# Gated linear attention into a gated MLP: three weight buffers, smaller batch buffers, ScalarE copies as fp32 words and a new order table

## The chip, the cores and the metric

The kernel runs on one core of a Trainium2 chip. A core has five engines with an instruction queue each: TensorE (PE in the profile; its weight loads are PEld), VectorE (DVE), ScalarE (ACT), GpSimd (POOL) and SyncE (SP), which here issues the transfers between HBM and SBUF. Matmul results go to PSUM, eight banks of 128 x 2 KB, which POOL does not read. The metric is the time of one execution on the device in microseconds (us); the kernel before takes 141.49 us, the median of three runs (141.25 to 141.82).

## The reference

Two stages in sequence, all inputs and outputs fp32. The shapes are batch 4, 8 heads, 768 steps, head width 48; then model width 384 and hidden width 1024.

```python
state = np.zeros((B, H, D, D))
for t in range(S):
    state = alpha[:, :, t, :, None] * state + np.einsum('bhd,bhe->bhde', k[:, :, t], v[:, :, t])
    y[:, :, t] = np.einsum('bhd,bhde->bhe', q[:, :, t], state)
x = y.transpose(0, 2, 1, 3).reshape(B, S, H * D)

h = np.maximum(x @ w_in, 0.0)
u, v = h[..., :512], h[..., 512:]
v_n = (v - mean(v)) / np.sqrt(var(v) + 1e-06)
v_s = np.einsum('ts,bsd->btd', w_spatial, v_n) + b_spatial[None, :, None]
out = (u * v_s) @ w_out
```

## The kernel before, in words

The steps are cut into 24 chunks of 128, six for each batch. Chunks 0 to 7 are worked on as four pairs (function `pair`), with even and odd steps interleaved; chunks 8 to 23 one at a time (function `first`). For a chunk or pair the work is:

- four loads, alpha, k, q and v (`ac`, `kc`, `qc`, `vc`; L432 for pairs, L637 for single chunks), each into one of three buffers;
- the logarithm of alpha on ScalarE (`lnp`, L443), its running sum as matmuls with triangular matrices (`cump`, L452, two matmuls for each half of a pair), the exponentials of the sum with both signs on ScalarE (L460, L469), k and q times these (`ktp`, L474, on POOL or VectorE; `qtp`, L481, on VectorE);
- transposes of k and q on TensorE (`tr`, L502, four 128-column matmuls each) and copies of the result from PSUM to the tile `kqT` on ScalarE or VectorE (`ev`; the copies of all steps are in the helper `copy`, L198 for ScalarE and L200 for the others);
- the update of the state from k and v on TensorE (`updq`, L536 and L544), the state itself on VectorE and POOL (`z`, `S`, `sb`);
- the scores (`sc`, L574), their masking on VectorE (`m`, L585 for pairs, L756 for single chunks), the output y as scores times v (`ya`, L601) plus q times state (`y`, L614);
- a copy of y to bf16 (`xs`), its transpose (`xt`, L365 for pairs, L389 for single chunks) and the copy to `xT` (`xe`). In the pairs' `xe` the copy also puts the interleaved steps back in order, by a strided access.

The MLP stage works on a batch. `second_v` makes the six v tiles (three matmuls of 512 columns each, relu on ScalarE, statistics on VectorE at L884 and L885, then `rs` and the normalisation `vn`, L916); `second_u` makes uT; `second_s` multiplies by the transposed spatial weights `w_spT` (six matmuls of 384 columns for each of eight groups, L967 adds the bias, L980 multiplies by u); `second_o` multiplies by w_out and stores. All its matmuls are recorded at L819, in the helper `mm`.

The weights arrive as fp32 in raw buffers (`raw_w`, `NRAW` = 2), through `fetch`: a load waits until the buffer used `NRAW` loads before has been cast to bf16. w_in comes as two loads, w_spatial as three, w_out as one. w_spatial is then transposed on TensorE (`wt`, L831) and copied to `w_spT` (`we`).

The order of all the work is fixed in advance: each operation is entered in a list with a number, and `replay` emits them as the string `PLAN` says. A word is an engine letter and a number, so the table also fixes which engine does an operation that two engines could do. Each engine works through its own queue in this order. Words like `P126:512:512:512` put filler in front of a matmul operation: matmuls of 512 fp32 columns each on the constant tile `junk` (L188) that write to the PSUM bank which the operation is about to overwrite. The old table has 3,768 such columns, all in the first 20 us: 1,216 ahead of the first `cump`, 1,536 ahead of the first `tr`, then 504 and 512.

PSUM banks are taken in turn by a counter (`bank`), so an operation also waits for the readers of the bank taken eight turns before. The lines that the change touches:

```python
    NRAW, NROW, KEEP = 2, 3, 11
...
                copy(eng, bt[b]["xT"][:, c].rearrange("p k (t two) -> p k t two", two=2),
                     st["xv"].rearrange("p k (two t) -> p k t two", two=2))
...
        d["xT"] = batch.tile([128, NCH, KS, C], BF16, name="xT")
        d["uT"] = batch.tile([128, NDS, S], BF16, name="uT")
        d["v_sb"] = batch.tile([128, NT, DH], BF16, name="v_sb", bufs=2)
```

The pool `batch` has three buffers where a tile does not name another number.

## Time and profile before

| | |
|---|---|
| median of three runs | 141.49 us (141.25 to 141.82) |
| span of the profiled execution | 144.3 us (the page gives no other time for it) |
| TensorE busy | 136.8 us, 95% |
| VectorE busy | 118.7 us, 82% |
| ScalarE busy | 106.8 us, 74% |
| POOL busy | 86.8 us, 60% |
| HBM traffic | 28.64 MB, 198 GB/s |
| chain that ended last, by engine | PE 78%, DVE 8%, ACT 5%, DMA 3% |

The profile is of one execution, and its span goes from the first to the last instruction; it is 2.8 us longer than the median of the runs. In a row of a group stand the line, the engine, the tiles (written <- read), the count, then the busy time, the mean of one in ns, and the idle time ahead of them with what ended it. In a row of the timeline stand the start, the duration, the engine and line, and in brackets the idle time before it. In a row of the stretches stand, after the stretch and its length, the busy time of PE, PEld, DVE, ACT and POOL with the number of instructions, then the granted TensorE clock, the share of the transfer engines and GB/s. A matmul's duration includes its way through the array and overlaps with the next; how fast TensorE gets on is read from the starts, or from the chain.

### The profile page before, as it was taken

Reading aid. Unit: us, or ns where it says so; the run is one execution under the profiler, and the core shown is the slowest. Engines: PE = TensorE matmul, PEld = TensorE weight load, DVE = VectorE, ACT = ScalarE, POOL = GpSimd, SP = SyncE. Lnnn points to the kernel's source line nnn. Section 1 sums busy time; section 2 is a strip of 40 time slices with the busy share of each in tenths; the row PEclk is TensorE's granted clock in tenths of the full one; section 3 lists DMA queues with packets and bytes.
Section 4 is the critical chain, followed back from the end, with each engine's and each line's share of the span. In section 5 each row is a group of like instructions: output and inputs, shape, how many; then the busy total and the mean of one; then the engine's idle time right before and its main releaser. Section 6 shows DMA issues by size and latency. Waiting matters only on the chain.

```text
span 144.3 us, 4963 instructions
## 1 busy us (share of the span) xinstructions
PE 136.8 (95%) x1915; PEld 84.2 (58%) x1915; DVE 118.7 (82%) x289; ACT 106.8 (74%) x278; POOL 86.8 (60%) x152
## 2 busy tenths in 40 slices
PE   7799999799799999999999999999999999999990
PEld 3334766656465765676556665665657666555560
DVE  7015798899999969899999999999979897987940
ACT  3473479899895879899997789998797698861031
POOL 6856179892709979981249789511599687002820
PEclk9999999999999999999999999999999999999998
DMA  4999999929899989999899899799999241090055
GB/s 108 321 326 351 282 250 325 344 58 259 181 269 191 300 164 182 205 181 214 169 211 222 175 174 185 152 204 196 212 239 227 66 172 55 0 354 28 5 191 191
DMA packets 89000, 28.64 MB, mean 198 GB/s; under 512 B 83728, under 2 KB 87440, under 8 KB 88976
## 3 DMA queue, kind: packets, MB, share of 16 engines
q1 hardware_dynamic: 88944, 28.32, 79.5%
q8 instruction: 15, 0.25, 0.7%
q14 instruction: 9, 0.07, 0.1%
q0 software_dynamic: 32, 0.00, 0.0%
HBM read 23.60 MB, written 4.72 MB: 196 GB/s over the span
## 4 chain that ended last, share of the span: by engine, by line
PE 78%; DVE 8%; ACT 5%; DMA 3%; issue 3%; SPq 0%; ACTq 0%; DVEq 0%
PE bank L819 47%; PE bank L188 4%; DMA ac<-in_alpha_dram 3%; PE bank L710 3%; PE bank L452 2%; PE bank L502 2%; PE bank L745 2%; PE bank L574 2%; DVE ptm L756 2%; PE bank L773 2%; PE bank L731 2%; PE bank L544 1%; DVE ptm L585 1%; PE bank L657 1%; PE bank L601 1%
## 5 line engine op out<-in xcount | busy, mean ns | idle before, releaser
L819 PE MATMUL bank<-w_spT,vn 128*128 128x384 bf16 x192 | 36.3, 326 | 0.1
L980 POOL TENSOR_TENSOR gT<-vsb,uT 128x384 bf16<-128x384 f32 x28 | 25.7, 927 | 11.7 <-DVE vsb L967 11.2
L335 POOL TENSOR_TENSOR state<-state,bc 128x192 f32<-128x192 f32 x20 | 10.3, 513 | 21.4 <-DVE state L328 6.2
L819 PEld LDWEIGHTS <-vn 128*128 128x128 bf16 x192 | 17.1, 97 | 10.2 <-issue 0.2
L756 DVE TENSOR_TENSOR ptm<-bank,mask 128x512 bf16<-128x512 f32 x32 | 20.8, 682 | 1.0 <-ACT xT L198 1.0
L819 PE MATMUL bank<-xT,w_in 128*128 128x384 bf16 x96 | 19.4, 326 | 0.0
L967 DVE TENSOR_TENSOR vsb<-bank,bsp_bc 128x384 f32<-128x384 f32 x31 | 16.7, 554 | 3.2 <-PE bank L819 2.8
L819 PE MATMUL bank<-w_in,xT 128*128 128x512 bf16 x72 | 18.8, 379 | 0.0
L198 ACT COPY kqT<-bank 128x512 bf16<-128x512 bf16 x24 | 13.6, 590 | 6.9 <-PE bank L502 4.4
L819 PE MATMUL bank<-w_out_sb,gT 128*128 128x384 bf16 (+1 forms) x100 | 18.4, 320 | 0.1
L681 POOL TENSOR_TENSOR kt<-kc,binv 128x384 bf16<-128x384 f32 x13 | 12.0, 927 | 6.6 <-ACT bc L676 2.7
L200 POOL CAST sbd<-state 64x192 bf16<-64x192 f32 x40 | 13.6, 341 | 2.1
L884 DVE BATCH_NORM_STATS2 stats<-v_sb 128x6 f32<-128x512 bf16 x20 | 13.6, 681 | 0.5 <-ACT v_sb L204 0.5
L204 ACT ACTIVATE v_sb<-bank 128x512 bf16<-128x512 f32 x20 | 11.9, 608 | 1.6 <-PE bank L819 1.6
L198 ACT CAST x_sb<-bank 128x384 bf16<-128x384 f32 x21 | 10.2, 493 | 3.5 <-PE bank L773 2.7
L819 PEld LDWEIGHTS <-w_in 128*128 128x128 bf16 x96 | 8.7, 97 | 6.0
L188 PE MATMUL bank<-junk 128*128 128x512 f32 (+2 forms) x16 | 11.1, 838 | 1.1 <-DVE halves_of L264 1.1
L200 DVE COPY kqT<-bank 128x512 bf16<-128x512 bf16 x24 | 9.2, 415 | 3.1 <-PE bank L502 2.3
L819 PEld LDWEIGHTS <-gT 128*128 128x128 bf16 x100 | 8.7, 97 | 5.1 <-POOL gT L980 0.2
L204 ACT ACTIVATE uT<-bank 128x384 bf16<-128x384 f32 x23 | 11.3, 495 | 0.3 <-PE bank L819 0.2
L198 ACT COPY xT<-bank 128x192 bf16<-128x192 bf16 (+1 forms) x27 | 9.1, 378 | 2.4 <-PE bank L365 1.5
L585 DVE TENSOR_TENSOR ptm<-bank,mask 128x512 bf16<-128x512 f32 x16 | 10.2, 682 | 0.7 <-PE bank L574 0.4
(128 smaller groups left out, 285.2 us busy)
## 6 DMA issues: line engine op xcount, KB each, us to landing
ac<-in_alpha_dram SPq DMA_DIRECT2D x16, 192.0 KB, 3.9
kc<-in_k_dram SPq DMA_DIRECT2D x16, 192.0 KB, 4.2
qc<-in_q_dram SPq DMA_DIRECT2D x16, 192.0 KB, 4.0
vc<-in_v_dram SPq DMA_DIRECT2D x16, 192.0 KB, 3.8
raw_w<-in_moe_w_spatial_dram SPq DMA_DIRECT2D x3, 768.0 KB, 4.5
out_dram<-raw_w SPq DMA_DIRECT2D x11, 192.0 KB, 2.0
out_dram<-o_sb SPq DMA_DIRECT2D x9, 192.0 KB, 1.9
ac<-in_alpha_dram SPq DMA_DIRECT2D x4, 384.0 KB, 5.5
```

What stands on the lines that cost most here:

```text
L188: nc.tensor.matmul(out=flat[:, 0:cols].rearrange("p (a b) -> p a b", a=4), lhsT=junk, rhs=junk[:, None, 0:n].to_broadcast([128, 4, n]), st ...
L198: nc.scalar.copy(out=out, in_=in_)
L200: ENG[eng].tensor_copy(out=out, in_=in_)
L204: nc.scalar.activation(out=out, in_=in_, func=AF.Relu)
L335: ENG[eng].tensor_tensor(out=st["state"], in0=st["state"], in1=st["bc"][:, :, None].to_broadcast([128, HP, D]), op=ALU.mult)
L585: nc.vector.tensor_tensor(out=st[f"ptm{par}"][:, s], in0=st[f"pt{s}{par}"], in1=mask2[:, par], op=ALU.mult)
L681: ENG[eng].tensor_mul(out=k_blocks(kt3)[:, :, :, 0:D], in0=quad(st["kc"]), in1=st["binv"])
L756: nc.vector.tensor_tensor(out=st["ptm"][:, s], in0=st[f"pt{s}"], in1=mask4, op=ALU.mult)
L819: return lambda ps: nc.tensor.matmul(out=out(ps), lhsT=lhsT(), rhs=rhs(), start=start, stop=stop)
L884: nc.vector.bn_stats(out=stats, in_=d["v_sb"][:, tt, :])
L967: nc.vector.tensor_tensor(out=hold["vs"], in0=ps[:, 0:TH], in1=bsp_bc[:, th, :], op=ALU.add)
L980: ENG[eng].tensor_tensor(out=bt[b]["gT"][:, dsl, cols], in0=hold["vs"], in1=bt[b]["uT"][:, dsl, cols], op=ALU.mult)
```

## The change

Six things change together.

1. The weights have three raw buffers instead of two (`NRAW` = 3).
2. `xT` and `uT` have two buffers instead of three. The v tiles are no longer held as six to a batch in two buffers but as pairs, in five buffers (`v_tile`, `NVS` = 5). The dependencies follow: a copy to `xT` now waits for the v and u matmuls of two batches before, a v tile for the normalisation of the pair five pairs before, uT for the products of two batches before. uT is taken at its first use.
3. Copies of transposed blocks on ScalarE (kqT, xT, w_spT) see both sides as fp32, half as many elements; on VectorE they stay bf16 (`copy_pairs`).
4. A second, permuted identity `ident_q` is made on POOL at the start. The pairs' `xt` uses it, so that the transpose puts the steps in order and the copy to `xT` is contiguous.
5. The bias row `b_sp_sb` lies in the memory of `w_spT`'s first row.
6. The order table is another one. It has 273 words for ScalarE (257 before), 244 for VectorE (257), 116 for POOL (119), and the same 300 for TensorE and 111 for SP. Of 48 kqT copies ScalarE has 38 (24 before). The filler has 2,496 columns: 960 ahead of the first `cump`, 128 and 256 ahead of the bias matmuls, 320 ahead of the first `tr`, then 128, 192, 128, 320 and 64.

```diff
 PLAN = """
-D0 S49 Q50 D7 D13 S109 Q110 G47 Q48 D11 S51 Q52 G9 D3 S55 Q56 D1 G8 D15 D17 G14 D6 D4 D2 D12 G16 S53 Q54 A57 S113 Q114
-G18 A117 P118:512:512:192 S111 Q112 P68 A119 P262 A69 P58 S19 Q20 P264 G71 A59 P128 A120 A60 G61 S115 Q116 A70 D62
-A129 D72 A265 D5 S178 Q179 A263 D122 A130 P126:512:512:512 D132 S180 Q181 G131 P76 P74 P64 P66 D75 G63 A65 D77 G73 D67
...
+S109 Q110 D0 D15 D3 G47 Q48 D6 D2 G16 D17 S49 Q50 D13 D1 D4 D5 S51 Q52 G14 D12 A117 S113 Q114 G9 P118:320:192:384:64
+A57 S53 Q54 P264:128 A119 P58 A120 P68 S55 Q56 A59 A69 D61 P262:256 A60 P128 G71 S111 Q112 D122 A263 A70 P126:320 G18
+A265 D72 S115 Q116 A129 D62 A130 P76 P74 D132 P66 A73 S178 Q179 G63 P64 D11 A127 G8 P78 A77 A67 A75 S182 Q183 G121 D80
...
 """
...
+    NVS = 5
...
-    NRAW, NROW, KEEP = 2, 3, 11
+    NRAW, NROW, KEEP = 3, 3, 11
...
+    def copy_pairs(eng, out, in_):
+
+        copy(eng, *((out.bitcast(FP32), in_.bitcast(FP32)) if eng == "ACT" else (out, in_)))
...
-    b_sp_sb = consts.tile([1, S], BF16, name="b_sp_sb")
     wsp_nat = [None] * NT
     w_spT = consts.tile([128, NT, NT, 128], BF16, name="w_spT")
+    b_sp_sb = w_spT[0:1, 0].rearrange("p n t -> p (n t)")
...
+    def x_users(b):
+
+        return got(*[("v", b - 2, t, "mm", 0) for t in range(NT)],
+                   *[("u", b - 2, ft, th, "mm", 0) for ft in range(NDS) for th in range(2)])
...
-                    nc.tensor.transpose(xv[:, ks, :], st["x_sb"][:, ks, :], ident)
+                    nc.tensor.transpose(xv[:, ks, :], st["x_sb"][:, ks, :], ident_q)
...
-                copy(eng, bt[b]["xT"][:, c].rearrange("p k (t two) -> p k t two", two=2),
-                     st["xv"].rearrange("p k (two t) -> p k t two", two=2))
+                copy_pairs(eng, bt[b]["xT"][:, c], st["xv"])
...
-                        copy(eng, st["kT"][:, par], hold["t"])
+                        copy_pairs(eng, st["kT"][:, par], hold["t"])
...
-        d["xT"] = batch.tile([128, NCH, KS, C], BF16, name="xT")
-        d["uT"] = batch.tile([128, NDS, S], BF16, name="uT")
-        d["v_sb"] = batch.tile([128, NT, DH], BF16, name="v_sb", bufs=2)
+        d["xT"] = batch.tile([128, NCH, KS, C], BF16, name="xT", bufs=2)
...
+    def v_tile(b, tt):
+
+        k = ("v_sb", tt // 2)
+        if k not in bt[b]:
+            bt[b][k] = batch.tile([128, 2, DH], BF16, name="v_sb", bufs=NVS)
+        return bt[b][k][:, tt % 2]
+
+    def v_users(b, tt):
+
+        n = b * NT // 2 + tt // 2 - NVS
+        return got(*[("vn", 2 * n // NT, 2 * n % NT + x) for x in range(2)]) if n >= 0 else []
...
+    def c_id(_):
+        make_identity(nc, ident)
+        nc.gpsimd.tensor_copy(
+            out=ident_q.rearrange("p (t a) -> p a t", a=2), in_=ident.rearrange("p (a t) -> p a t", a=2))
```

On SP the loads of the start change their order. Before: alpha of pair 0, alpha 1, k 0, v 0, q 0, q 1, k 1, the second half of w_in, v 1, the four loads of pair 2, alpha 3, the first half of w_in, q 3, k 3, then w_spatial with the loads of chunks 8 and 9. After: alpha 1, alpha 0, k 0, q 1, q 0, v 0, k 1, v 1, the four loads of pair 2, alpha 3, the second half of w_in, q 3, the first half of w_in, k 3, two of the three loads of w_spatial, q of chunk 8, v 3.

On TensorE the old order has the first two v groups after the first chunk's `xt`, ahead of pair 2's transposes; the new order has pair 2's transposes, scores and updates first and the v groups after. Of the last operations, the old table has both halves' last copies of the output on ScalarE and a 96 KB store as the last transfer; the new one splits the last copies over ScalarE and VectorE, and the last transfer has 192 KB.

More of the change, by code (lines that the diff above doesn't have):

```diff
@@ L210 @@
     ident = consts.tile([128, 128], BF16, name="ident")
+    ident_q = consts.tile([128, 128], BF16, name="ident_q")
     mask4 = consts.tile([128, 4, 128], BF16, name="mask4")
@@ L867, in evac @@
             if not on_act:
[L868 removed]
+                relu(eng, v_tile(b, tt), ps)
                 return
             nc.scalar.activation(
[L871 removed]
+                out=v_tile(b, tt), in_=ps, func=AF.Relu, accum_out=d["sums"][:, 0, tt:tt + 1])
         Q = 1000.0 + 100 * b
         group(("v", b, tt), mms, 0.22, made[("xe", b * NCH + tt)] + made[("w_in", 1)], Q + tt, evac,
[L875 removed]
+              {"ACT": 0.61 if on_act else 0.48}, None, v_users(b, tt), parts=1)
         def bn(_):
@@ L916, in vn @@
                     nc.vector.tensor_scalar(
-                        out=d["vn"][:, t, :], in0=d["v_sb"][:, t, :],
+                        out=d["vn"][:, t, :], in0=v_tile(b, t),
                         scalar1=d["mvs"][:, t, 0:1], scalar2=d["rstd"][:, t:t + 1],
@@ L925, in vn @@
                 nc.gpsimd.tensor_scalar(
-                    out=d["vn"][:, t, :], in0=d["v_sb"][:, t, :], scalar1=d["rstd"][:, t:t + 1], scalar2=nb,
+                    out=d["vn"][:, t, :], in0=v_tile(b, t), scalar1=d["rstd"][:, t:t + 1], scalar2=nb,
                     op0=ALU.mult, op1=ALU.add)
@@ L938, in evac @@
         def evac(eng, ps):
+            if "uT" not in bt[b]:
+                bt[b]["uT"] = batch.tile([128, NDS, S], BF16, name="uT", bufs=2)
             relu(eng, bt[b]["uT"][:, ft, th * TH:(th + 1) * TH], ps[:, 0:TH])
```

120 lines of the change are left out of this document (59 added, 61 removed).

## The prediction

> **What bounds the kernel now.** I read the busy times by stretch first, then the chain that ended last, then the single instructions of the start. The columns are PE, PEld, DVE, ACT and POOL busy.
>
> ```profile
> 6.40:16.90 10.50, 10.50 (x57) 4.63 (x57) 3.90 (x11) 4.73 (x11) 5.49 (x8) 1.00 1.14 331
> 16.90:42.50 25.60, 23.61 (x523) 16.08 (x520) 24.04 (x53) 22.58 (x56) 16.19 (x30) 1.00 0.83 239
> 42.50:140.80 98.30, 98.04 (x1342) 61.46 (x1332) 88.03 (x208) 75.88 (x208) 60.20 (x97) 1.00 0.77 174
> ```
> ```profile
> 6.38 1.44 PE bank L452 x4
> 7.82 0.43 PE bank L848
> ...
> 9.42 0.75 PE bank L452 x2
> 10.17 4.25 PE bank L188 x6
> 14.43 1.12 PE bank L502 x20
> 15.55 0.90 PE bank L188 x2
> ...
> 17.35 0.18 PE bank L536 x8
> 17.53 0.51 PE bank L544 x32
> 18.03 0.35 PE bank L574 x16
> ...
> 123.54 17.18 PE bank L819 x105
> ```
>
> Three regimes follow. From 42.5 us, where the spatial matmuls (L819, from w_spT and vn) begin, to 140.8 us TensorE is full: the last 105 matmuls take 17.18 us, 164 ns each. From 16.9 to 42.5 VectorE is the tight one, 24.04 of 25.60 us, and TensorE has holes of 2 us. Before 16.9 the chain is a latency chain in which TensorE is kept busy with filler: L188, matmuls on `junk` whose result nobody reads, stands on it with 4.25 and 0.90 us.
>
> The filler's length matters, for these rows show TensorE at half rate in the first stage:
>
> ```profile
> 1.06 4.42 PE L188 MATMUL bank<-junk 128*128 128x512 f32 x6 [1.06 <-DVE halves_of L264]
> 6.97 0.84 PE L452 MATMUL bank<-la,le_pair 128*128 128x384 bf16 x2
> 28.94 0.49 PE L452 MATMUL bank<-la,le_pair 128*128 128x384 bf16 x2
> ```
>
> The same two matmuls take 0.84 us at 6.97 and 0.49 at 28.94, though the granted clock is 1.00 throughout. The first filler, 1,216 columns by the order table, takes 4.42 us, 3.6 ns a column; the one at 15.55, 504 columns, 0.90 us, 1.8 ns a column. So the full rate comes between 10.2 and 14.4 us, during the second filler of 1,536 columns (at 3.6 ns it would be 5.5 us; it took 4.25, so it turned at about 13).
>
> **The change part by part.** *Copies as fp32 words.*
>
> ```profile
> L198 ACT COPY kqT<-bank 128x512 bf16<-128x512 bf16 x24 | 13.6, 590 | 6.9 <-PE bank L502 4.4 <-PE bank L710 2.1 <-DVE w_row L200 0.4
> L200 DVE COPY kqT<-bank 128x512 bf16<-128x512 bf16 x24 | 9.2, 415 | 3.1 <-PE bank L502 2.3 <-ACT o_sb L198 0.5
> L198 ACT COPY raw_w<-bank 128x384 f32<-128x384 f32 x9 | 4.4, 484 | 0.8 <-PE bank L819 0.7 <-issue 0.2
> L198 ACT COPY raw_w<-bank 128x192 f32<-128x192 f32 x1 | 0.3, 325 | 0.0
> L198 ACT COPY xT<-bank 128x192 bf16<-128x192 bf16 x19 | 5.3, 335 | 0.9 <-PE bank L389 0.9
> ```
>
> On ScalarE 192 elements take 325 ns as fp32 and 335 as bf16, 384 fp32 take 484: time goes by elements, 0.83 ns each, not bytes. A 512-element copy becomes 256 words: 325 + 64 x 0.83 = 378 ns instead of 590. VectorE keeps its form and 415 ns. The order table uses that: of 48 kqT copies ScalarE takes 38 (24 before), VectorE 10. ScalarE: 38 x 378 - 24 x 590 = +0.2 us, VectorE -14 x 415 = -5.8 us; with the other moved operations I count ScalarE -4.4, VectorE -3.1, POOL -3.3 us over the run. After 42.5 us this is worth nothing by itself: TensorE hides it. If words were no cheaper, ScalarE would have +8 us instead (a rival).
>
> *Transposes with ident_q.* Same number of matmuls, and the pair chunks' xT copy becomes contiguous. It costs POOL one 128x128 copy at the start; nearest is this POOL row, 661 ns for 512 elements, so between 0.17 (128 elements at its rate) and 0.66 us; I take 0.3, nearer the small end by size:
>
> ```profile
> L241 POOL TENSOR_SCALAR_AFFINE_SELECT mask<-mask 64x512 bf16<-64x512 bf16 x4 | 2.6, 661 | 0.1
> ```
>
> It is hidden: POOL's first ktp needs ScalarE's exponential, after 8 us. POOL now also makes one mask (two selects, 1.3 us) ahead of the triangles that the first cumulative sum needs; they were done at 4.1 us and will be at about 4.5, under the 5.1 at which it can start; without that cover 0.4 us.
>
> *Buffers.* Five pairs of v tiles instead of six, xT and uT for two batches instead of three: a v tile now waits for the normalisation (vn) five pairs back, xT for the matmuls of two batches back. By both order tables at least 27 us of TensorE work lie between, so nothing; without that distance ScalarE's v copy, and the copies queued behind it, would wait. The bias row shares w_spT's space and is read some 30 us before w_spT is written: nothing.
>
> *Third weight buffer and the loads' order.*
>
> ```profile
> 18.46 1.29 SPq L1084 DMA_DIRECT2D raw_w<-in_moe_w_in_dram  x1
> 31.77 0.37 SPq L1084 DMA_DIRECT2D raw_w<-in_moe_w_spatial_dram  x1
> raw_w<-in_moe_w_in_dram SPq DMA_DIRECT2D x2, 768.0 KB, 6.5
> ```
>
> The second w_spatial load held SP's queue until 31.77 for a free buffer, with the last v of the pairs behind it; now it waits for the first w_in casts, on VectorE at about 25, so the queue moves on some 5 us sooner. In return the first w_in load goes from 8th to 14th, behind pair 2's four loads and pair 3's alpha. It is issued at about 18.46 less its own share of the stream (768 KB at 331 GB/s, 2.4 us) = 16.1 and lands 6.5 later, 22.6, ahead of its casts. Pair 2's inputs come 2.4 us earlier.
>
> *The new order at the start.* The filler is 2,496 columns instead of 3,768, in smaller pieces.
>
> ```profile
> 4.24 0.84 ACT L443 ACTIVATE la<-ac 128x768 bf16<-128x768 f32 x1 [2.21 <-DMA ac<-in_alpha_dram]
> 5.48 0.84 ACT L443 ACTIVATE la<-ac 128x768 bf16<-128x768 f32 x1 [0.40 <-DMA ac<-in_alpha_dram]
> 16.89 1.29 DVE L585 TENSOR_TENSOR ptm<-bank,mask 128x512 bf16<-128x512 f32 x2 [0.33 <-issue]
> ```
>
> The alpha pair that TensorE needs first is now loaded first: its logarithm ends at 5.08, not 6.32. Then, at half rate: sums of that pair 0.72 (half of the L452 x4) to 5.8; filler of 128 at 3.6 ns 0.46, bias 0.43, to 6.7; the other pair's four 1.44 to 8.1; filler 256 0.92, bias 0.43, two sums 0.75, to 10.2; filler 320 1.15, to 11.4. There the first transposes start, 14.43 before. Five of them, 0.22 at full rate (1.12/5), 0.44 at half, end at 13.6; the update matmuls 0.18 + 0.51 at 14.3; then ScalarE's small exponential and its last copy, 0.2 + 0.38, 14.9; the first scores 0.35, 15.3: the first mask on VectorE at 15.3 instead of 16.89, 1.6 us sooner. ScalarE carries all of these copies, four were VectorE's: at 0.38 they keep up.
>
> From the first mask to the first spatial matmul VectorE then has, by the order table and the spacing of each group in the trace, 13 masks (2.48/4 = 0.62) 8.1, six statistics 0.80 each 4.8, four qt 2.05, four vn 1.9, four state sums 1.3, two u 1.0, two copies 0.7, two w_in casts 0.9, x_sb 0.53, kt 0.52, w_spT 0.3: 22.1 us, against 24.04 busy in 25.60 before. The rows for masks and vn:
>
> ```profile
> 28.86 2.48 DVE L585 TENSOR_TENSOR ptm<-bank,mask 128x512 bf16<-128x512 f32 x4 [0.39 <-PE bank L574]
> 35.28 1.92 DVE L916 TENSOR_SCALAR vn<-v_sb,mvs,rstd 128x512 bf16<-128x512 bf16 x4
> ```
>
> With the same share of holes it takes 22.1 x 25.60/24.04 = 23.5 us, 2.1 less. So the spatial matmuls start between 1.6 us earlier (only the first mask's lead survives) and 1.6 + 2.1 = 3.7 us. I take 2.5, near the middle, because the second half of each pair's masks now waits for scores that stand later in TensorE's order, which may eat about half of the 2.1. Late next is TensorE itself.
>
> *From there on* the matmuls are the same: nothing, within 2 us either way. *The tail:*
>
> ```profile
> 140.75 0.70 ACT L198 COPY raw_w<-bank 128x384 f32<-128x384 f32 x2 [0.17 <-PE bank L819]
> 141.67 0.41 SPq L1011 DMA_DIRECT2D out_dram<-raw_w  x1
> out_dram<-raw_w SPq DMA_DIRECT2D x2, 96.0 KB, 1.7
> out_dram<-raw_w SPq DMA_DIRECT2D x11, 192.0 KB, 2.0
> ```
>
> Two ScalarE copies in 0.70 become one of 0.48 beside one of VectorE, -0.2; the last store has 192 KB instead of 96, +0.3: nothing.
>
> **Sum.** Span 144.3 - 2.5 = 141.8. The profiled span stands 2.8 us over the median of 141.49 (page and runs give no other time for that execution), so I scale: 2.5 x 141.49/144.3 = 2.45, 139.0 us.
>
> **The rivals.** *The clock stays at half.* Without the 1,536 columns there is no unbroken stretch of 4.25 us; if the full rate came only at about 20 us, the work from 13 to 20 would go at half: up to the first y that is two updates (1.4), three transposes (0.7), three scores (1.05) and a pair's sums (0.7), 3.8 us at full rate, and so 3.8 us more; 142.8. It decides if the rate turns after about 18 us. For it: 4.42 us of filler at 1.06 did not turn it. Against it: 6.4 to 11.4 is now as closely filled as before, and when TensorE is late it is busy, which turns it. The Trainium skill, "TensorE: Matmul & The Clock Gate", Part 1, speaks for it: the full clock needs a busy window of about 3.4 us, and the window runs freely. By that rule any gap in the window can cost another one, and the sum would be the rival's 142.8 rather than 139.0. The trace agrees in so far as 4.42 us of filler, followed by a gap, left the next matmuls at half rate. Chance 0.16.
>
> *VectorE takes it all back.* The masks, statistics and vn before the first spatial matmul wait for each other; if holes of 2.5 us open there, 141.4. For it: VectorE is the tight engine there. Against: it has 2 us less to do. Chance 0.12.
>
> *ScalarE becomes the bound.* If words cost what bf16 elements did, 212 ns each: its 14 kqT copies before the spatial matmuls are 3.0 us, six pair xT and four w_spT copies at 155 ns 1.5; 4.5 on an engine with 25.60 - 22.58 = 3.0 to spare: the lead of 2.5 lost and 1.5 over, 143.0, and with 24 more such copies later, each 0.2 where TensorE has no slack, up to 145; 144. Against: the 192-element rows. Chance 0.08.
>
> *The middle gains too.* These are the best spacings of a chunk's matmuls:
>
> ```profile
> 53.04 0.19 PE bank L389 x6
> 53.23 0.23 PE bank L710 x16
> 54.71 0.33 PE bank L745 x8
> 58.33 0.20 PE bank L731 x8
> 60.15 0.17 PE bank L767 x4
> 60.32 0.20 PE bank L773 x8
> ```
>
> Sixteen chunks at 1.3 us and 0.1 for their sums are 22.5 us; 365 matmuls at 164 ns 59.9; 54 at 217 ns (0.65 for three) 11.7: 94 of the 98.3 us after 42.5. If half of the 4 us goes, 137.0. For it: loads now lead their first reader by 4.1 us or more of TensorE work, 2.8 before. Chance 0.12.
>
> **How the numbers follow.** The forecast has 0.52, own range 137.8 (all 3.7) to 140.5 (a little over 1). Half a per cent, 0.7 us, is what a measurement can tell from no change. Faster: 0.50 + 0.12 + 0.02 = 0.64; within: 0.02 + 0.08 = 0.10; slower: 0.16 + 0.08 + 0.02 = 0.26. The range 136.6 to 143.0 reaches to the middle's gain and to the half clock, and leaves out ScalarE's case and both ends.
>
> **What would show it.** Right: first transposes near 11.4, first mask near 15.3, first spatial matmul near 40; kqT copies on ScalarE at about 380 ns; from there TensorE full for 98 us. Wrong: L502 or L574 at twice their spacing after 15 us; kqT copies near 590; TensorE idle for VectorE or ScalarE after 45 us; the first w_in load landing after 25.

## The result, and the profile after

| | before | after |
|---|---|---|
| median of 20 runs each, same chip | 141.82 us (141.25 to 147.89) | 142.63 us (141.63 to 144.03) |
| ratio after / before | | 1.0064, 95% interval 1.0040 to 1.0088 |
| runs under 142 us, over 144 us | 13, 5 | 4, 1 |

By the ratio the change makes the kernel slightly slower: 0.64%, where 139.0 us had been forecast. The ratio leaves out executions more than 1.5% above the fastest of their kernel, five of before's (those over 144 us) and two of after's, so it is not the quotient of the two medians, which are over all runs. The mean of all 20 runs hardly differs (142.61 and 142.71 us): before is mostly near 141.5 us and sometimes near 145, after lies between. The profiled execution of after has a span of 140.0 us and a time of 141.79; in every run with a span on record the time is 1.7 to 1.9 us more than the span.

The page after, its busy times and the groups that answer to those of before (columns as there):

```profile
PE 132.6 (95%) x1923; PEld 84.2 (60%) x1923; DVE 118.9 (85%) x276; ACT 101.7 (73%) x294; POOL 84.5 (60%) x150
...
L199 ACT COPY kqT<-bank 128x256 f32<-128x256 f32 x38 | 13.3, 384 | 3.9 <-PE bank L720 3.2
...
L936 DVE TENSOR_SCALAR vn<-v_sb,mvs,rstd 128x512 bf16<-128x512 bf16 x24 | 11.1, 491 | 1.0 <-ACT rstd L929 0.9
```

The word copies cost what was forecast, 384 ns against 378. VectorE's busy time has not fallen (118.7 before): vn costs 491 ns where it was 430.

TensorE's timeline of after at the start. It is the counterpart of the rows of L188, L452 and L502 before (now L189, L462, L512):

```profile
1.05 3.67 PE L189 MATMUL bank<-junk 128*128 128x320 f32 x8 [1.05 <-DVE junk L1073]
5.13 0.32 PE L462 MATMUL bank<-la,le_pair 128*128 128x384 bf16 x1 [0.40 <-ACT la L453]
...
6.68 0.49 PE L462 MATMUL bank<-la,le_pair 128*128 128x384 bf16 x2
...
8.71 0.40 PE L512 MATMUL bank<-ident,qt 128*128 128x128 bf16 x4
```

Two sums of a pair take 0.49 us already at 6.68, so the full rate is there before; the profile of before had 0.84 at 6.97. The first transposes start at 8.71, not at 11.4 as forecast.

The stretches of after, cut at the first mask (12.8) and at the first spatial matmul (36.6); columns as in the prediction:

```profile
6.00:12.80 6.80, 5.47 (x91) 3.80 (x90) 4.36 (x10) 6.31 (x19) 4.31 (x8) 1.00 1.17 325
12.80:36.60 23.80, 23.33 (x485) 16.18 (x486) 22.07 (x50) 22.07 (x61) 15.40 (x29) 1.00 1.04 309
36.60:136.30 99.70, 99.21 (x1341) 61.17 (x1337) 89.88 (x201) 70.18 (x213) 60.80 (x99) 1.00 0.76 172
```

VectorE is busy for 22.07 of 23.80 us between the two marks, as forecast (22.1 of 23.5). TensorE then takes 99.7 us to its last matmul, where the profile of before had 98.5 between the same two marks. And the transfers' share is 1.04 in the middle stretch: there is no room left in it. The answers to the load rows of before:

```profile
raw_w<-in_moe_w_spatial_dram SPq DMA_DIRECT2D x3, 768.0 KB, 8.0
...
raw_w<-in_moe_w_in_dram SPq DMA_DIRECT2D x2, 768.0 KB, 7.6
```

These took 4.5 us (w_spatial, by the same view of before between 16 and 43 us) and 6.5 before.

The end of after, all engines:

```profile
126.36 5.53 PE L827 MATMUL bank<-w_spT,vn 128*128 128x384 bf16 x33
...
128.34 2.66 POOL L1003 TENSOR_TENSOR gT<-vsb,uT 128x384 bf16<-128x384 f32 x3 [11.02 <-DVE vsb L990]
...
130.15 1.26 DVE L1003 TENSOR_TENSOR gT<-vsb,uT 128x384 bf16<-128x384 f32 x1
131.33 0.55 DVE L983 TENSOR_TENSOR gT<-bank,uT 128x384 bf16<-128x384 f32 x1
...
134.34 1.97 PE L827 MATMUL bank<-w_out_sb,gT 128*128 128x384 bf16 x15 [0.34 <-DVE gT L1003]
```

One product on VectorE takes 1.26 us; three of POOL's run from 128.34 to 131.00, the last of them beside it. VectorE's next product, which reads PSUM and starts when POOL's are done, takes 0.55. Four microseconds after the slow one TensorE waits 0.34 us for VectorE's last product.

### The profile page after: what moved, and what is told of

It reads as the page before. It is cut to its first block, busy times and chain, and to the rows that moved or that the text cites. A ratio compares the mean times of both kernels' runs of the same rounds, so it can differ in the third digit from the quotient of the medians.

```text
span 140.0 us, 4956 instructions
## 1 busy us (share of the span) xinstructions
PE 132.6 (95%) x1923; PEld 84.2 (60%) x1923; DVE 118.9 (85%) x276; ACT 101.7 (73%) x294; POOL 84.5 (60%) x150
## 3 DMA queue, kind: packets, MB, share of 16 engines
HBM read 23.60 MB, written 4.72 MB: 202 GB/s over the span
## 4 chain that ended last, share of the span: by engine, by line
PE 83%; ACT 6%; DMA 3%; DVE 2%; issue 2%; POOL 1%; SPq 0%; POOLq 0%; DVEq 0%; ACTq 0%
PE bank L827 54%; PE bank L720 3%; DMA ac<-in_alpha_dram 3%; PE bank L755 3%; PE bank L667 2%; PE bank L783 2%; PE bank L584 2%; PE bank L512 2%; PE bank L741 2%; PE bank L777 2%; PE bank L399 2%; PE bank L376 1%; ACT bank L479 1%; PE bank L839 1%; ACT binvp L470 1%
## 5 line engine op out<-in xcount | busy, mean ns | idle before, releaser
L1003 POOL TENSOR_TENSOR gT<-vsb,uT 128x384 bf16<-128x384 f32 x25 | 22.5, 914 | 13.8 <-DVE vsb L990 13.3
L341 POOL TENSOR_TENSOR state<-state,bc 128x192 f32<-128x192 f32 x20 | 11.1, 553 | 18.3 <-DVE state L336 5.2
L990 DVE TENSOR_TENSOR vsb<-bank,bsp_bc 128x384 f32<-128x384 f32 x31 | 16.2, 552 | 2.8 <-PE bank L827 1.1
L691 POOL TENSOR_TENSOR kt<-kc,binv 128x384 bf16<-128x384 f32 x14 | 13.2, 946 | 6.4 <-ACT binv L679 3.9
L199 ACT COPY kqT<-bank 128x256 f32<-128x256 f32 x38 | 13.3, 384 | 3.9 <-PE bank L720 3.2
L904 DVE BATCH_NORM_STATS2 stats<-v_sb 128x6 f32<-128x512 bf16 x20 | 13.6, 682 | 0.3 <-ACT v_sb L209 0.2
L199 ACT CAST x_sb<-bank 128x384 bf16<-128x384 f32 x19 | 9.0, 486 | 6.2 <-PE bank L783 4.1
L936 DVE TENSOR_SCALAR vn<-v_sb,mvs,rstd 128x512 bf16<-128x512 bf16 x24 | 11.1, 491 | 1.0 <-ACT rstd L929 0.9
L209 ACT ACTIVATE uT<-bank 128x384 bf16<-128x384 f32 x21 | 10.2, 498 | 1.7 <-PE bank L827 1.7
L701 DVE TENSOR_TENSOR qt<-qc,bank 128x384 bf16<-128x384 f32 x16 | 8.7, 550 | 1.8 <-ACT bank L696 1.0
L679 ACT ACTIVATE binv<-bank 128x384 bf16<-128x384 f32 x16 | 7.9, 493 | 3.1 <-PE bank L670 2.6
```

The costliest lines, as they stand in the source:

```text
L199: nc.scalar.copy(out=out, in_=in_)
L209: nc.scalar.activation(out=out, in_=in_, func=AF.Relu)
L341: ENG[eng].tensor_tensor(out=st["state"], in0=st["state"], in1=st["bc"][:, :, None].to_broadcast([128, HP, D]), op=ALU.mult)
L691: ENG[eng].tensor_mul(out=k_blocks(kt3)[:, :, :, 0:D], in0=quad(st["kc"]), in1=st["binv"])
L904: nc.vector.bn_stats(out=stats, in_=v_tile(b, tt))
L936: nc.vector.tensor_scalar(out=d["vn"][:, t, :], in0=v_tile(b, t), scalar1=d["mvs"][:, t, 0:1], scalar2=d["rstd"][:, t:t + 1], op0=ALU.subt ...
```

## The experiments

The theory after this comparison: the profile that the forecast was summed against showed an execution of before in which TensorE's full rate came late; the median execution has it early, so there is little to win at the start. The rivals: the gain is there, but late loads eat it; or the new order loses it in its middle and tail; or the words, the buffers or the filler cost something by themselves. All times are medians with the range and number of runs; the ratio is to runs of before on the same chip, with its 95% interval.

### When TensorE's full rate comes

*e1_before_again* and *e9_before_third* are the kernel before, unchanged.

> The kernel before, profiled a second time. Theory A (the profile of before that the prediction was made from shows a late execution: TensorE at half rate until 13 us): in this execution the full rate is there by about 5 us, the pair of L452 matmuls takes 0.49 us instead of 0.84, the second filler ends near 11.5 instead of 14.4, and the span is 139.5 to 140.5, some 4 us under the 144.3 of the first profile, at a time near 141.5. Theory B (the profiler lengthens this kernel's execution): span again near 144.3 with the half rate until 13 us while the time is 141.5. Ratio to itself 1.000.

> The kernel before once more. Theory A: the profile catches an execution with the full rate by about 6.5 us; its first spatial matmul is then near 38 instead of 42.5 and its span near 139.7. If it is again a late one, the span is 144.

Measured: 145.20 us (142.94 to 146.05, 6), ratio 1.0171 (1.0080 to 1.0262); and 143.81 us (142.12 and 145.49). The first is the same kernel against itself: on that chip the other runs of before are six of 141.27 to 141.77, one of 143.22 and four of 145.23 to 145.67. So a single kernel has two groups of times, 4 us apart, and an interval of a few runs of it can miss 1. TensorE at the start of e1:

```profile
1.06 4.42 PE L188 MATMUL bank<-junk 128*128 128x512 f32 x6 [1.06 <-DVE halves_of L264]
...
6.91 0.84 PE L452 MATMUL bank<-la,le_pair 128*128 128x384 bf16 x2
...
9.90 3.62 PE L188 MATMUL bank<-junk 128*128 128x512 f32 x4
```

Half rate again until about 13 us, and the profiled execution took 146.05 us, a member of the upper group. e9 is alike (0.84 at 6.99; 145.49 us). So neither expectation came as written: the profiler does not lengthen the execution, since time and span are long together, but no early execution of this kernel was caught either. The first profile of before, with a span of 144.3, the same as e1's, is such an execution of about 146 us, not one of 141.5.

The kept traces also record from when the full clock was granted: 13.4 us after the first instruction in before, 13.6 in e1, 14.0 in e9, but 5.1 in after. The rows of the stretches show 1.00 for the time before that record too.

*e5_before_longer_filler* is before with more filler ahead of the first `cump`.

```diff
-P118:512:512:192
+P118:512:512:512:64
```

> The kernel before with 1,600 columns of first filler instead of 1,216, so that TensorE has no gap between the filler and the first sums. Theory A (the times of 144 to 146 us of this kernel are executions in which the full rate comes only during the second filler): those executions vanish, all times near 141.5. Rival (they come from somewhere else, transfers for instance): about a third of the times stays at 144 to 146.

Measured: 142.61 us (141.60 to 147.14, 12), ratio 0.9979 (0.9926 to 1.0031). In its profile the two sums take 0.49 us at 7.29, and the first mask comes at 14.39 instead of 16.89. Eight of the twelve times are under 143, but three are over 144, where all had been expected near 141.5; the median is not told apart from before's. The profiled execution, with its early rate, took 143.71. The longer filler takes away the late rate in the trace, and the time has another cause of scatter, below.

*e12_after_no_filler* is after without any filler.

```diff
-P118:320:192:384:64
+P118
...
-P126:320
+P126
```

> The new kernel without any filler matmul. Rival of the prediction 'the clock stays at half': TensorE runs at half rate until the first long matmuls at 24 us, the first mask comes at 17 to 18 us and the first spatial matmul at about 40, the time 145 to 147. If the half rate does not matter because the start waits for other engines, the time stays at 142 to 143.

Measured: 146.44 us (146.00 to 146.69, 4), ratio 1.0248 (1.0184 to 1.0312). TensorE in it:

```profile
6.95 0.84 PE L462 MATMUL bank<-la,le_pair 128*128 128x384 bf16 x2
...
13.53 0.64 PE L584 MATMUL bank<-kqT 48*64 48x128 bf16 x16 [0.56 <-ACT kqT L199]
...
18.13 0.42 PE L584 MATMUL bank<-kqT 48*64 48x128 bf16 x16
```

Scores take 0.64 us at 13.53 and 0.42 at 18.13: without filler the half rate lasts to 17.7 us by the clock record. The median is 3.8 us above after's, on another chip; the expected 145 to 147 us came, but not all by the expected way. The first mask is at 14.28 (17 to 18 expected) and the first spatial matmul at 38.88, 2.3 us later than in after; the other loss lies behind it (102.3 us to the last matmul against 99.7), where POOL waits 2.2 us each for late kc and vc. The four runs lie within 0.7 us.

### The parts of the change alone

*e2_before_words* is before with the word copies, `ident_q` and the bias row in `w_spT`'s memory, with the old order and the old buffers.

```diff
+                copy_pairs(eng, bt[b]["xT"][:, c], st["xv"])
...
+    b_sp_sb = w_spT[0:1, 0].rearrange("p n t -> p (n t)")
```

> The old order, old buffers, with parts 3, 4 and 5 alone: ScalarE copies as fp32 words, ident_q, the bias row in w_spT. Its 24 kqT copies on ScalarE should take 380 instead of 590 ns. Theory 'ScalarE is not the bound': ratio 0.997 to 1.001, since TensorE hides it. Rival 'the start is bound by copies': about 1 us faster, 0.993.

Measured: 143.74 us (141.38 to 145.72, 6), ratio 1.0025 (0.9938 to 1.0112). kqT copies at 376 ns, but no gain that six runs with an interval of 1% to either side can tell. That TensorE hides them in the old order, as forecast, is argued. The execution in the profile (143.29 us) has the early rate, from 5.6 us on.

*e3_after_plain_copies* is after with bf16 copies on ScalarE.

```diff
-        copy(eng, *((out.bitcast(FP32), in_.bitcast(FP32)) if eng == "ACT" else (out, in_)))
+        copy(eng, out, in_)
```

> The new kernel with ScalarE's copies of transposed blocks as bf16 again (590 ns). If the words carry the new order, ScalarE gets 8 us more work over the run, and the first spatial matmul starts 2 to 4 us later: ratio to the old kernel 1.02 to 1.04. If ScalarE has slack everywhere, the ratio stays at 1.006.

Measured: 149.99 us (148.89 to 150.48, 6), ratio 1.0567 (1.0509 to 1.0626). Its ScalarE group and two rows of TensorE:

```profile
L199 ACT COPY kqT<-bank 128x512 bf16<-128x512 bf16 x38 | 21.4, 605 | 4.2 <-PE bank L720 3.2
```
```profile
13.41 0.42 PE L584 MATMUL bank<-kqT 48*64 48x128 bf16 x16 [1.46 <-ACT kqT L199]
...
16.86 1.14 PE L462 MATMUL bank<-la,le_pair 128*128 128x384 bf16 x3
```

The copies are 8.1 us dearer over the run (21.4 against 13.3), TensorE waits 1.46 us for one, and three sums at 16.86 take 1.14 us where the same three take 0.66 in after: the rate had fallen back, by the clock record from 14.6 to 18.0 us. The first spatial matmul comes at 40.70, 4.1 us later than in after, and as much again is lost behind it (103.8 us to the last matmul against 99.7). The new order stands on the words; the old one does not need them.

*e8_after_old_order* is after with the old order table: three raw buffers, smaller batch buffers and words, none of the new order. *e11_new_code_old_order_long* is the same with 1,536 columns of filler ahead of the first `cump` instead of 1,216.

```diff
-P118:512:512:192
+P118:512:512:512
```

> The new code and buffers with the old order table: parts 1 to 5 without part 6. If the order makes the difference, the time is that of the kernel before or less by what cheaper ScalarE copies save: 140.5 to 141.5, with the old kernel's two groups of times. If buffers or words cost something (waits on five pairs of v tiles, say), it is slower than 142.

> The new code with the old order (third buffer, words, v pairs) and a first filler of 1,536 columns. From the lowest time of the old order in the new code, 140.92: the common times at 140.9 to 141.6, fewer at 144 and above, ratio 0.985 to 0.998 against the kernel before. If the early weight loads of the third buffer push the chunk loads back, the times scatter over 141 to 144 as before.

Measured, e8 and e11: 143.79 us (140.92 to 148.69, 8), ratio 0.9876 (0.9764 to 0.9987); and 142.92 us (141.26 to 145.92, 12), ratio 0.9944 (0.9889 to 0.9999). TensorE and VectorE in e8:

```profile
6.76 0.49 PE L462 MATMUL bank<-la,le_pair 128*128 128x384 bf16 x2
...
8.48 2.74 PE L189 MATMUL bank<-junk 128*128 128x512 f32 x6
11.53 0.62 PE L512 MATMUL bank<-ident,qt 128*128 128x128 bf16 x8 [0.31 <-DVE qt L491]
```
```profile
14.16 1.29 DVE L595 TENSOR_TENSOR ptm<-bank,mask 128x512 bf16<-128x512 f32 x2 [0.33 <-POOL vbp L201]
```

This is the old order in an execution with an early rate: the second filler takes 2.74 us instead of 4.46, the first mask comes at 14.16 instead of 16.89, the first spatial matmul at 37.75 instead of 42.55. None of that needs the new order. Both intervals end just below 1, but with runs from 140.9 to 148.7 us and on chips where before itself had medians of 143.61 and 144.73; I do not call either a faster version. e8's median missed the expected 140.5 to 141.5, and e11's times scatter, as the second theory in its expectation had it.

e11's profile is of its slowest execution, 145.92 us, and yet the full rate is there by 4.8 us and the first spatial matmul at 37.54. The time goes in the middle, here TensorE, POOL, and a stretch with the columns of the prediction:

```profile
83.59 0.28 PE L720 MATMUL bank<-ident,qt 64*128 64x64 bf16 x8
86.53 0.31 PE L720 MATMUL bank<-ident,kt 64*128 64x64 bf16 x8 [2.66 <-POOL kt L691]
```
```profile
85.57 0.91 POOL L691 TENSOR_TENSOR kt<-kc,binv 128x384 bf16<-128x384 f32 x1 [4.67 <-DMA kc<-in_k_dram]
```
```profile
86.68:90.10 3.42, 3.20 (x33) 1.38 (x30) 1.70 (x5) 1.80 (x6) 3.18 (x6) 0.50 1.07 204
```

POOL waits 4.67 us for a late kc and TensorE 2.66 us for POOL, and behind that wait the granted clock is 0.50 for 3.4 us. A late load thus costs twice, and an execution of the upper length need not have a late start. The mean granted clock of this execution is 0.988; nine runs of the unchanged kernel on these chips, at 144.74 to 146.40 us, have the same mean. That they too fell back once is likely, but not shown: none of them was profiled.

### Whether loads eat the gain

In *e6_after_wide_loads*, *e7_before_wide_loads* and *e10_before_wide_long* the loads of single chunks read runs of 1,536 bytes, not of 192, from the same tensors as they lie; the values land in other places, so these are tests and no versions. e10 has e5's filler too.

```diff
-                nc.sync.dma_start(out=t, in_=src[b, :, t0:t0 + C, :].rearrange("h s d -> s h d"))
+                nc.sync.dma_start(
+                    out=t.rearrange("p h d -> p (h d)"),
+                    in_=src[b].rearrange("h s d -> (h s d)")[c * C * DM:(c + 1) * C * DM].rearrange("(p x) -> p x", p=C))
```

> The new kernel in which the loads of the single chunks (8 to 23) fetch the same number of bytes as runs of 1,536 bytes instead of 192; the values land in other places, so what is computed from them is not the reference's. Theory D (the new order starts earlier, but the transfers cannot come earlier, and their late landings give the lead back after 37 us): no DVE, ACT or POOL wait for a load after 30 us, the stretch from the first spatial matmul to the last matmul falls from 99.8 to about 97.5 us, the time to 139.5 to 140.5 and the spread of the times shrinks. Rival (the middle is TensorE's own work): time stays at 142 to 143.

> The same loads in the kernel before; what is computed from them is not the reference's either. Theory D: the old order starts later and has its transfers in time, so it gains less than the new one: 0.5 us or less, 141.0 to 141.5. Rival (transfers cost both the same): it falls as much as the new kernel does, to 139.5.

> The kernel before with both suspected causes of scatter taken away: 1,600 columns of first filler and the loads of single chunks as runs of 1,536 bytes (the output is not the reference's). If late full rate and late transfers are all there is, every time is within 141.3 to 142.2. If a third cause exists, some times stay above 143.

Measured: e6 141.89 us (141.56 to 143.62, 12), ratio 0.9975 (0.9924 to 1.0026); e7 141.76 us (141.34 to 145.37, 12), ratio 0.9924 (0.9876 to 0.9972); e10 141.59 us (141.37 to 142.42, 10), ratio 0.9936 (0.9897 to 0.9975). A stretch in the middle, first of after, then of e6; the last two columns are the transfers' share and GB/s:

```profile
80.00:90.00 10.00, 10.00 (x157) 6.05 (x153) 9.12 (x24) 8.99 (x31) 8.30 (x14) 1.00 1.02 207
```
```profile
80.00:90.00 10.00, 10.00 (x154) 6.10 (x153) 9.31 (x23) 8.79 (x31) 8.49 (x14) 1.00 0.61 204
```

At the same 205 GB/s the short runs fill the transfer engines (1.02), the long ones take 0.61 of them. e6's median is 0.74 us below after's, which was measured on another chip, and eleven of twelve runs are under 142.8. But 139.5 to 140.5 us and about 97.5 us behind the first spatial matmul had been expected, and it takes 99.4: late loads are the smaller part of what the new order loses there. e7 (141.0 to 141.5 expected) has eight runs under 142.2 and four from 142.89 to 145.37; the slowest, which was profiled, has the late rate (from 13.5 us). e10, with the long runs and the long filler, has all ten runs within 141.37 to 142.42: with either alone (e5, e7) the scatter stays, with both it is gone. And with wide loads the old order (e10) is not slower than the new one (e6).

*e4_after_more_filler* is after with 1,088 and 192 columns ahead of the first two places instead of 960 and 128.

```diff
-P118:320:192:384:64 ... P264:128
+P118:512:512:64 ... P264:192
```

> The new kernel with the first filler 1,088 columns in three pieces instead of 960 and 192 instead of 128 ahead of the first bias matmul, so that TensorE has no gap from 1.05 us to the first sums. Theory A (the new kernel's spread of 141.6 to 144.0 is the time at which the full rate comes): the times gather near the lowest, median 141.8 to 142.2, ratio 1.000 to 1.004. Rival (the spread has another cause, such as transfers): median 142.6, ratio 1.006, and the same spread.

Measured: 143.82 us (143.01 to 145.51, 6), ratio 1.0133 (1.0073 to 1.0192). Its full rate is there by 5.7 us, about as in after, and it is no faster; no time gathers near 141.6, as the theory had expected. The chain that ended last:

```profile
16.41 7.28 DMA raw_w<-in_moe_w_in_dram
23.71 0.77 DVE w_in L201 x2
...
42.74 5.72 DMA qc<-in_q_dram
49.05 0.55 DVE qt L701
...
97.80 4.94 DMA qc<-in_q_dram
```

Three loads stand on it, of 7.28, 5.72 and 4.94 us. How long a load is under way in that crowded stretch differs from execution to execution, and it decides here more than the filler.

### Where the new order gives its lead back

*e13_after_other_tail* moves one product in VectorE's queue behind the next one; *e14_after_wide_other_tail* has the same tail and e6's loads.

```diff
-D1099 P1114 D1100 G1112 P1122 D1127 P1117
+D1099 P1114 G1112 P1122 D1127 D1100 P1117
```

> The new kernel with one product of the tail moved in VectorE's queue: the product (gT) that takes 1.26 us beside three of POOL's goes behind the next one, which reads PSUM. If VectorE's and POOL's products slow each other in the tail, its gT falls from 1.26 us to under 0.8, TensorE's wait of 0.34 us for gT near 134 us goes or shrinks to under 0.1, and the end of the last matmul comes 0.3 to 0.6 us earlier after the first spatial matmul (99.75 us before this edit, 99.2 to 99.5 with it). If the 1.26 us has another cause (the product waits for its inputs while it is counted as busy), it stays near 1.2 us in its new place and the tail keeps its length. In time both expect a difference below what a measurement can tell: 142.0 to 143.0 us.

> The same tail in the new kernel with wide loads (the single chunks' loads as runs of 1,536 bytes, so that the values land in other places and the output is not the reference's). With late loads out of the way the new order's lead of 0.8 us at the first spatial matmul should show in the end if the tail alone takes it back: 141.3 to 141.6 us, against 141.89 with the old tail. If the lead is lost between the first spatial matmul and the tail, 141.7 to 142.0 us.

Measured: e13 144.12 us (142.40 to 145.69, 6), ratio 1.0079 (1.0004 to 1.0154); e14 141.82 us (141.09 to 143.07, 6), ratio 0.9976 (0.9911 to 1.0041). The tail of e14:

```profile
130.03 0.55 DVE L985 TENSOR_TENSOR gT<-bank,uT 128x384 bf16<-128x384 f32 x1
130.50 0.91 DVE L1005 TENSOR_TENSOR gT<-vsb,uT 128x384 bf16<-128x384 f32 x1
...
131.72 4.12 PE L829 MATMUL bank<-w_out_sb,gT 128*128 128x384 bf16 x28
```

The product now takes 0.91 us instead of 1.26, not under 0.8 as expected (three of POOL's end at 130.99, so it still has one beside it for half a microsecond), and TensorE runs 28 matmuls without the wait of 0.34. From the first spatial to the last matmul pass 98.95 us, 99.40 in e6. So the two engines do slow each other, and this one place is worth 0.45 us, between two profiles. The median, 141.82 against 141.89, does not show it: six runs that scatter by 2 us cannot. It lies where the expectation had put a loss ahead of the tail (141.7 to 142.0), not where the tail alone would take the lead back (141.3 to 141.6).

e13's profile is of another kind. Its start:

```profile
1.05 3.68 PE L189 MATMUL bank<-junk 128*128 128x320 f32 x8 [1.05 <-DVE junk L1073]
...
7.30 0.85 PE L462 MATMUL bank<-la,le_pair 128*128 128x384 bf16 x2
...
10.69 0.68 PE L512 MATMUL bank<-ident,qt 128*128 128x128 bf16 x8
```

Half rate up to 10.3 us: the new order has late executions too. It loses less by them: the first spatial matmul comes at 38.47, 1.5 us later than in e6, where the old order loses 4.1 (41.83 in e7 against 37.75 in e10, which differ in the first filler alone). Then kc and qc come late (waits of 2.6 and 2.3 us on POOL and VectorE), and the execution takes 145.69 us, so that e13 cannot test the tail.

## Why the prediction was wrong

The marks of the profiled executions, in us, from the timelines and, for the full rate, the clock records:

| | full rate from | first mask | first spatial matmul | from there to the last matmul ended | span |
|---|---|---|---|---|---|
| before (first profile) | 13.4 | 16.89 | 42.55 | 98.5 | 144.3 |
| e1, before again | 13.6 | 16.93 | 42.49 | 98.5 | 144.3 |
| e9, before, third time | 14.0 | 17.20 | 41.89 | 98.5 | 143.7 |
| e7, before, wide loads | 13.5 | 16.86 | 41.83 | 98.5 | 143.6 |
| e2, before, words | 5.6 | 14.25 | 39.50 | 98.7 | 141.5 |
| e5, before, longer filler | 7.3 | 14.39 | 38.43 | 100.2 | 141.9 |
| e8, new code, old order | 5.4 | 14.16 | 37.75 | 100.1 | 141.1 |
| e11, the same, longer filler | 4.8 | 13.81 | 37.54 | 103.3 | 144.1 |
| e10, before, wide loads, longer filler | 4.1 | 13.71 | 37.75 | 98.5 | 139.6 |
| after | 5.1 | 12.89 | 36.57 | 99.7 | 140.0 |
| e4, after, more filler | 5.7 | 12.94 | 37.04 | 101.8 | 142.6 |
| e6, after, wide loads | 5.6 | 12.82 | 36.97 | 99.4 | 140.1 |
| e14, the same with the other tail | 5.0 | 12.82 | 36.89 | 98.95 | 139.6 |
| e13, after, other tail | 10.3 | 14.06 | 38.47 | 101.7 | 143.9 |

**The step that failed: "the full rate comes between 10.2 and 14.4 us".** I read it as a property of the kernel; it is one of the profiled execution. The forecast gain of 2.5 us at the first spatial matmul was against 42.55, and the old order reaches 37.54 to 39.50 by itself in the five profiles in which the rate is early (e2, e5, e8, e10, e11). Against 37.75, where e8 and e10 have it, the new order's lead is 0.8 to 1.2 us (36.97 in e6 and 36.57 in after). That the unchanged kernel's median runs are of the early kind is argued, not shown: the profiles of it that I have are all of the late kind (times of 145.5 to 146 us). The argument is its lower group of times, 141.3 to 141.8, beside the early traces of its neighbours: no profile here takes less than 98.5 us from the first spatial to the last matmul and the old order 3.3 us more to the end, so a span near 139.7 leaves no room for a first spatial matmul after 38.

**The sum.** "The profiled span stands 2.8 us over the median, so I scale" was the place to see it. Scaling by 141.49/144.3 took the excess for a uniform one of 2%; it lay in the first 17 us. If the excess is taken off where it lies, nothing much of the gain is left: 42.55 less 2.5 was 40.05, and every early execution is already below that.

**The start itself** was worked out about right. VectorE's list is 22.07 us in 23.80 (22.1 in 23.5 forecast), the first w_in load is issued at 16.14 (16.1), and in after everything comes earlier than forecast because the rate does: first mask 12.89, not 15.3; first spatial matmul 36.57, not about 40. In the kind of execution that I had assumed the start gains more than forecast: e13 against e1, both late (10.3 and 13.6 us), has its first mask 2.9 and its first spatial matmul 4.0 us earlier. But e13 then takes 101.7 us instead of 98.5, and of the 4.0 us only 0.4 is left in the span, so even there the sum would not have come true.

**"Late next is TensorE itself", and "from there on nothing, within 2 us either way".** The sign was left open and the loss was not taken into the sum. Old order 98.5 us from the first spatial matmul on; new order 99.4 without late loads, 99.7 with. The balance of e6 against e10, where neither rate nor loads disturb: 0.8 earlier at the first spatial matmul, 0.9 longer to the last one, and 0.4 more from there to the end (140.1 - 136.37 = 3.7 us against 139.6 - 136.26 = 3.3), together 0.5 us later, as the spans say. These are two profiles, on two chips. Half of the 0.9 is the tail's product (e14). About 0.2 us is no loss but work on the other side of the mark: all sixteen single chunks' running sums lie behind it in e6 (the first at 37.46), fifteen in e10 (the first at 36.52, ahead of 37.75). The rest I have not located.

**The loads.** "The loads now lead their first reader by 4.1 us or more" counted from a queue that moves on, not from transfers that are full. The third buffer does let SP go on (w_in's load at the time forecast), but the transfers' share is 1.04 from the first mask to the first spatial matmul, so w_spatial takes 8.0 us to land, and whatever starts earlier waits for data: in the old order too, the early executions e5 and e8 take 1.6 us more after the first spatial matmul than the late ones, and e11 takes 4.8 more. (The early e2 takes 98.7, but comes to that matmul 1.8 us later than e8; why is not followed up.) With wide loads (e10) nothing waits for a load behind it, and the early execution takes 98.5 us like the late ones. After's median is 0.74 us lower with wide loads, across two chips.

**Words:** size right (384 ns), and worth nothing that e2 could measure alone, while the new order needs them (e3). **VectorE -3.1 us over the run:** wrong, +0.2. Durations were carried over from before, but in after more of VectorE's products, kt, vn and casts lie beside POOL's work, as the last section shows: by count times the change of the mean, 1.5 us on vn, 0.8 on the products, 0.6 on kt and 0.1 on a cast, together 2.9 of the 3.3 us. **The tail, "-0.2 and +0.3: nothing":** it cost 0.4, and the wait in front of it 0.45.

**The rivals.** The half clock did occur (e13: to 10.3 us; e12: to 17.7 us), but not until 18, and not in after's profile. That any gap in the window can cost another one was too strict: TensorE was idle for 0.40 us from 4.72 on in after, and the full clock came at 5.1. The middle did not gain. ScalarE did not become the bound with words; without them TensorE waits for its copies and the rate falls back as well (e3, 150 us where 144 had been given). VectorE's taking it all back came nearest to the result, though not where I had put it: not ahead of the first spatial matmul but in the tail. That 142.63 lies inside the range of 136.6 to 143.0, and next to the 142.8 of the half clock, is luck: neither case is what after's profile shows.

What stays open: why the same queue gets the full rate early or late; the share of late loads in the 0.64%, beyond the 0.74 us between two medians on two chips; and some 0.25 of the 0.9 us. That the new order's lead over the median execution of before was so small is by the argument above, not by a profile of that execution.

## What to carry to other kernels

Before a profile is used as the base of a sum, compare its span with the median of the runs; where they differ, find the stretch in which they differ, and sum against the execution that the median stands for, never by scaling. Warm-up filler should be long enough that the full rate does not hang on luck, and a kernel with two groups of times should be judged by its groups. Where transfers are full, an earlier issue is not an earlier landing: shorten what a load costs the transfer engines (longer runs in the tests here) before giving it another buffer.

## What the runs showed that I had not expected

**The early and the late rate.** With the same 1,216 columns of filler (4.42 us) and a gap of 0.81 to 0.97 us behind it, the next matmuls came at half rate in four profiles (before, e1, e7, e9) and at full rate in two (e2, e8). With 1,536 columns or more it was full rate in three of three (e5, e10, e11); with the new order's 960 it was early in four profiles (after, e3, e6, e14) and late in one (e13). The granted clock in the rows of the start is 1.00 in both kinds, so it does not tell them apart; the durations and the clock record do. In the record every stretch at full clock that ends in the trace lasts a whole multiple of 3.41 us (3 and 38 times in e3, 24 and 16 in e11, 37 to 40 elsewhere), and both falls back to half inside the work last 3.41 us; they follow on an idle TensorE, 1.46 us of it in e3 and 2.66 us in e11. The Trainium skill, "TensorE: Matmul & The Clock Gate", Part 1, has the activity window of about 3.4 us run freely, and says that the same kernel therefore gets its full clock after a varying number of matmuls. The traces agree with the window and with the varying moment, 4.1 to 14.0 us here with filler. By that rule, as an estimate, a stretch of 4.42 us holds a whole window in (4.42 - 3.41)/3.41, three cases in ten, and one of 5.5 us or more in six of ten. For the new order's 3.67 us the same estimate gives less than one in ten, where four of five were early, so a window need not be busy to its end: after's, from 1.67 to 5.08, has 0.35 us idle. Nor is a window that looks busy enough: in before, e1, e7 and e9 the 3.41 us ahead of the one that raised the clock (6.6 to 10.0 in before) count as busy throughout and did not raise it. What counts as busy stays open. The page puts the cost of the ramp under 1% of a kernel; here e7 and e10, which differ in the first filler alone, have spans 4.0 us apart (143.6 and 139.6), 3%, and the measurement decides.

**VectorE beside POOL.** The view of one tile or line, with the smallest, median and largest duration in ns; first products and normalisations of after, then the products of before:

```profile
L1003 DVE TENSOR_TENSOR gT<-vsb,uT x6: 544/548/1259, 44.1 to 133.7; 128x384 bf16<-128x384 f32 x6
```
```profile
L936 DVE TENSOR_SCALAR vn<-v_sb,mvs,rstd x24: 381/407/1056, 31.2 to 125.1; 128x512 bf16<-128x512 bf16 x24
```
```profile
L980 DVE TENSOR_TENSOR gT<-vsb,uT x3: 548/548/549, 115.1 to 135.9; 128x384 bf16<-128x384 f32 x3
```

The products that read two SBUF tiles go from 548 to 1,259 ns when POOL is at work. Over all sixteen kept traces, 38 such products that start while POOL is idle take 543 to 551 ns. Twenty-two start with 0.2 us or more left of an instruction of POOL's: 21 of them end 0.41 to 0.42 us after it (the one of 1,259 ns began with 0.85 us left), and beside the other, in e3, POOL's instruction began at the same time and took 1.33 us instead of 0.95. With vn, 29 of 30 end 0.14 to 0.15 us after POOL's. The 338 masks that start so, which read PSUM and one SBUF tile, take 656 to 693 ns, as they do beside an idle POOL. The Trainium skill, "SBUF — State Buffer", "SBUF: two separate sides", says that VectorE and GpSimd share one pair of ports as an exclusive lock, and names VectorE's instructions with two SBUF inputs among those that need it; whoever comes second waits for the whole instruction of the other. The traces agree. The forecast's durations for VectorE had no such term.

**Nearly the same bandwidth, another share.** Runs of 192 bytes fill the transfer engines at 207 GB/s, runs of 1,536 bytes take 0.61 of them at 204 GB/s.
